# Transfer times in a hand-planned order: one queue accounted by bytes, big loads in pieces, deeper weight staging, gate operands split in place

## The chip, the core and the metric

The kernel runs on one core of one Trainium2 chip. The metric is the device time of one execution in microseconds; the time before is the median of three runs. Engines are named as in the profile: PE is the matrix engine, ACT and DVE are the two elementwise engines, POOL does almost nothing here, and SP issues all the transfers, on one queue and in program order. Every engine works through its own list of instructions in order, so an instruction that waits holds back all that stands behind it on that engine.

## The reference

The input x is 4 sequences of 3072 rows with 256 channels. Three stages follow one another.

```
# 1: mixing in the frequency domain, along the sequence
X  = rfft(x, axis=1)
Yr = Xr @ w_r - Xi @ w_i + b_r ;  Yi = Xr @ w_i + Xi @ w_r + b_i
Y  = soft_threshold(Yr, 0.01) + 1j * soft_threshold(Yi, 0.01)
x  = irfft(Y)
# 2: two dense layers, 256 -> 2048 -> 256 (w_in, w_out)
h = x @ w_in ;  x = (h * tanh(softplus(h))) @ w_out
# 3: channel mix over the token before, 256 -> 1024 -> 256 (w_k, w_v), gate (w_r of its own)
x_prev = x shifted by one row
k = relu((mu_k*x + (1-mu_k)*x_prev) @ w_k)
r = sigmoid((mu_r*x + (1-mu_r)*x_prev) @ w_gate)
out = r * ((k*k) @ w_v)
```

The weights of stages 2 and 3 come as 64-bit floats and are decoded on the chip.

## The kernel before, in words

**Number format.** A matrix product is done in three passes: each operand is split into a rounded high part (a copy on ACT) and a low part (a subtraction on DVE), and high×high, high×low and low×high are added up. All elementwise helpers have one line each: `tt` (L201) and `stt` (L204) on DVE, `act` (L207) on ACT, `mm` (L210) on PE.

**Part 1** (stage 1, L650) is 48 steps u, 12 for each sequence b. A step runs a forward transform (`emit_F`, tile xps), the channel mix (`emit_M`, yps) and an inverse transform (`emit_I`, bps) on PE, with the evacuations `post_F` (xh, xl), `post_M` (yb) and `post_I` (bs, stored to b_dr) between them. The combining of 24 rows before and after lies on DVE: `f1_ops` ahead, `f3_ops` behind. `f3_ops` (L330) loads one half of a sequence from b_dr into the tile g (1536 KB, L334 to L337), runs about 46 DVE operations in place and stores to y_dr. For sequence 0 it runs inside part 1, for the others in part 2.

**Weight staging.** In steps 36 to 47 the weights of stage 2 are loaded in 16 pieces of 512 KB (`raw_piece`, L497; tile raw, three buffers), decoded on DVE and ACT (`decode`, L503) and split. A pipeline (`Weights`, L591) takes two pieces in a step: `vec` issues the DVE part, `sca` the ACT part and the load of a later piece, so that at most `depth` pieces lie loaded and not yet begun (L841: three at the start; L875, L880: two later). The first eight pieces belong to w_in; each pair of them is widened to seven matrices for a seven-product scheme (`pair_pieces`, L558), split into a staging tile (yc in the trace) and stored to h_dr by two stores of 896 KB (L583), 14 rows of 512 bytes in each partition. The last eight belong to w_out and stay on the chip (wo). The weights w_k are staged the same way in steps 6 to 14 (tile wst).

**Part 2** (stages 2 and 3, L908) works on 12 superblocks J of 1024 tokens. Stage 2 has 8 groups of hidden columns for each superblock (96 groups), stage 3 has 4 (48 groups). A group (`group`, L932) makes seven products of 128×512 tiles in banks x, z, c, d, sums on DVE (k), activations on ACT (h) and low parts on DVE (l); the second layer's product of a group (`unit_H`, `unit_K`; banks a and v) follows one group later. The 384 loads of first-layer weights (`load_ring`, L645; tile wr) go into two rings of four tiles; a load waits until the group two earlier has used its tile.

**The order** of part 2 is written by a planner (`Plan`, L97). Each step has an engine, a hold time, a due time and the steps it needs. The planner keeps one clock for each engine; when an engine is free in its account, it emits of the steps whose needs are met in that account the one with the earliest due time, early or not. A step is done after its hold, a hand-over time (`AFTER`, L101) and, for transfers, a landing time:

```
AFTER = {"PE": 0.2, "ACT": 0.19, "DVE": 0.16, "POOL": 0.3, "SP": 0.0, "-": 0.0}
last = add("SP", 0.1, t0, load, prev, land=9.0)      # f3_job: 1536 KB
```

A transfer thus holds SP for 0.1 or 0.2 us in the account, whatever its size. The account decides only the order; on the chip the engines wait for each other by semaphores. The steps on SP are: `load_ring`; the source tiles of the next superblock (`moving`, L1054: ysrc or xsrc, 1 MB by two transfers in one step, then four sums on DVE and seven splits); the loads and stores of `f3_job` (L1078); the stores of the shifted mixes (L1143, xk_dr and xr_dr through four tm buffers); the decoding of w_v and the gate's weight (dec, L1154 on, five pieces in sequence); the fetch of the weights of stage 3 (L1194, wk and wv); the gate's operand (`gate_prep`, L1254: 1 MB into xrf, split into xr); and the stores of the result. The gate (`gate`, L1280, bank z, tile r) runs four times a superblock, one in each group of stage 3, and in the first superblock two in group 2 and two in group 3.

Of the kernel before, what the change touches and what calls it, by code (L numbers as in the profile page):

```python
# [25 lines left out]
NB = 4  # L26
# [70 lines left out]
class Plan:  # L97
# [3 lines left out]
    AFTER = {"PE": 0.2, "ACT": 0.19, "DVE": 0.16, "POOL": 0.3, "SP": 0.0, "-": 0.0}  # L101
# [67 lines left out]
def tile_fft_mix_moe_channel_mix(  # L169
# [160 lines left out]
    def f3_ops(b, h):  # L330
# [3 lines left out]
        def load():  # L334
            G = g_p.tile([128, 32, 128], F32, tag="g", name="g")
            st["G"] = G
            nc.sync.dma_start(out=G[:, 0:24, :], in_=b_dr[b][h].rearrange("p t (r f) -> p (t r) f", r=2))  # L337

# [138 lines left out]
    def load_mix(h):  # L477
        raw = pools["st"].tile([128, 2, 256], F32, tag="raw", name="wraw", bufs=3)
# [18 lines left out]
    def raw_piece(src):  # L497
        raw = pools["st"].tile([128, 512, 2], I32, tag="raw", name="raw", bufs=3)
# [59 lines left out]
    def pair_pieces(w, dst, i, m, field, stage):  # L558
# [8 lines left out]
        def second():  # L567
            a0, v0, v1, a2, v2, a1 = decode(raw_piece(w[:, 256 * (i + m):256 * (i + m) + 256]),
                                            lambda: f["s"][:, 4:7:2, :], lambda q: [])
            s = lambda k: f["s"][:, k, :]  # L570

# [4 lines left out]
            def highs():  # L576
                t = f["t"] = stage()
                return [lambda: act(t[:, 0:4, 0, :], f["s"][:, 0:4, :], ACTF.Copy),
                        lambda: act(t[:, 4:7, 0, :], f["s"][:, 5:8, :], ACTF.Copy)]

            def lows():
                t = f["t"]
                put = lambda g: nc.sync.dma_start(  # L583
                    out=dst[2 * i + g], in_=t.rearrange("p m s f -> p (m s) f")[:, :, 128 * g:128 * g + 128].bitcast(F32))
                return [lambda: tt(t[:, 0:4, 1, :], f["s"][:, 0:4, :], t[:, 0:4, 0, :].bitcast(F32), SUB),
                        lambda: tt(t[:, 4:7, 1, :], f["s"][:, 5:8, :], t[:, 4:7, 0, :].bitcast(F32), SUB),
# [30 lines left out]
    def load_y(j):  # L617
        b, o = divmod(j, 3)
        t = src_p.tile([128, 8, 512], F32, tag="src", name="ysrc")
        for h in range(2):  # L620
            nc.sync.dma_start(out=t[:, 6 - 2 * h:8 - 2 * h, :].rearrange("p i f -> p (i f)"),
                              in_=y_dr[b][h, :, 8 * o:8 * o + 8, :].rearrange("p n f -> p (n f)"))
        return t
# [26 lines left out]
    def part1():  # L650
        with ExitStack() as es:
# [169 lines left out]
            for u in range(NU):  # L821
# [9 lines left out]
                if u == NU - NT - 1:  # L831
                    mv[0] = big.tile([128, 2, 7, 512], F32R, tag="big", name="yc")
                    flat = mv[0].rearrange("p a b f -> p (a b f)")
                    half = [flat[:, 3584 * i:3584 * i + 3584].rearrange("p (m s f) -> p m s f", m=7, s=2) for i in range(2)]
# [6 lines left out]
                    wq.load(3)  # L841
# [3 lines left out]
                elif PARK_AT[0] <= u < PARK_AT[1]:  # L845
                    dec = 1
                    if u == PARK_AT[0]:
                        wfield = src_p.tile([128, 2, 8, 256], F32, tag="src", name="wsrc")
                        todo = []
                        for i in range(2):  # L850
                            todo += pair_pieces(w_k, k_dr, i, 2, lambda i=i: wfield[:, i],
                                                lambda: g_p.tile([128, 7, 2, 256], F32R, tag="g", name="wst"))
# [21 lines left out]
                if dec:  # L874
                    emit(wq.sca(2))  # L875
                if u > 1:
                    post_I(u - 2)
                if dec == 2:
                    emit(wq.vec())
                    emit(wq.sca(2))  # L880
# [8 lines left out]
                if b == NB - 1:  # L889
                    if t == 6:  # L890
                        ysrc = load_y(0)
# [6 lines left out]
            while wq.busy():  # L898
                emit(wq.vec())
                emit(wq.sca(2))  # L900
# [7 lines left out]
    def part2():  # L908
        with ExitStack() as es:
# [76 lines left out]
            def outs_of(second, off, f32_of, hi_of, unit_of, cost):  # L986
# [65 lines left out]
            out_H = outs_of(units, 0, f32_H, None, unit_H, 1.362)  # L1052

            def moving(key, b0, pace, load, old, *prev):  # L1054
# [4 lines left out]
                def get():  # L1059
                    tl["s"] = load()  # L1060
                ld = add("SP", 0.2, b0, get, *prev, land=7.0)
# [33 lines left out]
            for J in range(NSB):  # L1095
# [5 lines left out]
                if J + 1 < NSB:  # L1101
                    old = [p for g in range(8) for p in prods[8 * (J - 1) + g]] if J else None
                    yprep[J + 1], src_reads = moving(J + 1, B0 + 8, 6.0, lambda J=J: load_y(J + 1), old,
                                                     src_reads, f3_of.get((J + 1) // 3))
# [269 lines left out]
```

## Time and profile before

| | |
|---|---|
| Median of 3 runs | 1937.7 us (1934.22 to 1941.81) |
| The profiled execution: time | 1939.15 us |
| The profiled execution: span of its instructions | 1937.4 us |
| PE busy, DVE busy, ACT busy | 1878.8, 1397.8, 1210.2 us |
| Granted PE clock, mean | 0.992 of full |
| Transfers | 255.66 MB, 41.8% of 16 DMA engines' time |

In views over time, the number after a start time is a duration, and brackets hold the idle time of that engine just before, with what ended it. Lines with SPq are the issuing of a transfer, not its duration. Part 1 runs to about 342 us, stage 2 to about 1345 us, stage 3 to the end.

### The profile page before, as it was taken

The page shows a single profiled execution, that of the slowest core. Times are in us where ns is not written, and L with a number is a line of the kernel's source. Part 1 is how long each engine was busy: PE and PEld are TensorE (multiplying, and loading weights), DVE is VectorE, ACT ScalarE, POOL GpSimd, SP SyncE. Part 2 cuts the span into 40 slices and gives each one's busy share as a digit, 9 for nine tenths or more (in the row PEclk, how much of TensorE's full clock was granted, in tenths as well). Part 3 has the DMA queues.
Part 4 walks back from the last instruction along what each step waited for, and adds up shares of the span by engine and source line. Part 5 has one row for each costly group of instructions (what it writes and reads, how often), then busy time and mean ns, then how long its engine had stood idle before and what let it go on. Part 6 is the DMA issues. An engine that isn't in the chain of part 4 may idle for free.

```text
span 1937.4 us, 26749 instructions
## 1 busy us (share of the span) xinstructions
PE 1878.8 (97%) x9654; PEld 1611.2 (83%) x9654; DVE 1397.8 (72%) x2565; ACT 1210.2 (62%) x2141; POOL 7.6 (0%) x16
## 2 busy tenths in 40 slices
PE   6999989898999998999999999999999999999999
PEld 5888877687878887778888888888899999999998
DVE  8999976697988895766747567575666666666654
ACT  2432276565657577875757667575777777777765
POOL 0000000000000000000000000000000000000000
PEclk9999999999999999999999999999999999999999
DMA  9455186456456554544434344353412222211201
GB/s 285 128 171 174 54 266 194 160 175 212 139 174 209 155 166 148 187 137 128 155 90 155 106 142 155 90 180 91 168 66 67 69 76 70 70 66 66 75 25 34
DMA packets 197539, 255.66 MB, mean 132 GB/s; under 512 B 15128, under 2 KB 126368, under 8 KB 196384
## 3 DMA queue, kind: packets, MB, share of 16 engines
q1 hardware_dynamic: 197408, 253.96, 41.8%
q8 instruction: 77, 1.26, 0.3%
q14 instruction: 54, 0.44, 0.1%
HBM read 177.35 MB, written 76.55 MB: 131 GB/s over the span
## 4 chain that ended last, share of the span: by engine, by line
PE 87%; DVE 4%; DMA 4%; ACT 4%; issue 1%; SPq 0%; ACTq 0%; DVEq 0%
PE a L210 25%; PE x L210 14%; PE v L210 13%; PE c L210 10%; PE yps L210 5%; PE z L210 5%; PE d L210 5%; PE zps L210 3%; PE bps L210 3%; PE xps L210 3%; DMA raw<-in_moe_w_out_dram 1%; DMA wr<-h_dr 1%; ACT L207 1%; DVE a L201 1%; ACT k L207 1%
## 5 line engine op out<-in xcount | busy, mean ns | idle before, releaser
L201 DVE TENSOR_TENSOR l<-k,h 128x512 fp32r<-128x512 f32 x576 | 385.3, 686 | 376.3 <-ACT h L207 203.6
L210 PE MATMUL a<-h,wo 128*128 128x512 f32 x1536 | 531.9, 390 | 0.0
L210 PEld LDWEIGHTS a<-h,wo 128*128 128x128 f32 x1536 | 289.5, 189 | 60.5
L210 PE MATMUL a<-l,wo 128*128 128x512 f32 x768 | 299.9, 391 | 5.8 <-DVE l L201 5.8
L210 PE MATMUL v<-wv,h 128*128 128x256 f32 x1536 | 278.2, 280 | 0.0
L207 ACT ACTIVATE c<-x 128x512 f32<-128x512 f32 x288 | 168.6, 586 | 157.8 <-PE x L210 153.4
L210 PEld LDWEIGHTS v<-wv,h 128*128 128x128 f32 x1536 | 247.5, 190 | 13.8
L210 PE MATMUL x<-yc,wr 128*128 128x512 f32 x864 | 244.8, 392 | 3.9 <-ACT c L207 3.5
L207 ACT ACTIVATE k<-k 128x512 f32<-128x512 f32 x288 | 177.1, 632 | 69.9 <-DVE k L201 67.7
L210 PE MATMUL v<-wv,l 128*128 128x256 f32 x768 | 215.3, 280 | 0.0
L210 PEld LDWEIGHTS x<-yc,wr 128*128 128x128 f32 x864 | 162.4, 189 | 40.8 <-ACT c L207 5.6
L207 ACT ACTIVATE k<-c 128x512 f32<-128x512 f32 x288 | 172.1, 598 | 33.6 <-PE c L210 18.0
L210 PE MATMUL c<-yc,wr 128*128 128x512 f32 x576 | 164.1, 393 | 13.1 <-DVE k L201 13.1
L207 ACT ACTIVATE d<-x 128x512 f32<-128x512 f32 x144 | 84.2, 585 | 146.8 <-PE x L210 146.8
L210 PEld LDWEIGHTS a<-l,wo 128*128 128x128 f32 x768 | 144.8, 189 | 36.3 <-DVE l L201 6.2
L210 PEld LDWEIGHTS v<-wv,l 128*128 128x128 f32 x768 | 144.6, 188 | 0.0
L207 ACT ACTIVATE h<-k 128x512 fp32r<-128x512 f32 x192 | 117.5, 629 | 42.4 <-DVE k L204 40.5
L210 PEld LDWEIGHTS c<-yc,wr 128*128 128x128 f32 x576 | 108.1, 189 | 38.5 <-DVE k L201 16.4
L201 DVE TENSOR_TENSOR k<-c,zs 128x512 f32<-128x512 f32 x144 | 99.1, 688 | 51.6 <-ACT c L207 48.6
L210 PE MATMUL x<-yc,wk 128*128 128x512 f32 x432 | 124.1, 396 | 0.0
L201 DVE TENSOR_TENSOR g<-g 128x128 f32<-128x128 f32 (+3 forms) x272 | 110.0, 432 | 1.4 <-DMA wr<-h_dr 0.4
L210 PE MATMUL bps<-im,yb 128*128 128x256 f32 x384 | 93.3, 387 | 10.5 <-DVE yb L204 10.5
(105 smaller groups left out, 2823.1 us busy)
## 6 DMA issues: line engine op xcount, KB each, us to landing
wr<-h_dr SPq DMA_DIRECT2D x288, 256.0 KB, 2.7
b_dr<-bs SPq DMA_DIRECT2D x48, 256.0 KB, 2.2
g<-b_dr SPq DMA_DIRECT2D x8, 1536.0 KB, 7.0
ysrc<-y_dr SPq DMA_DIRECT2D x24, 512.0 KB, 4.6
wr<-h_dr SPq DMA_DIRECT2D x96, 128.0 KB, 2.1
xk_dr<-tm SPq DMA_DIRECT2D x48, 256.0 KB, 3.1
xr_dr<-tm SPq DMA_DIRECT2D x48, 256.0 KB, 3.2
xsrc<-xk_dr SPq DMA_DIRECT2D x24, 512.0 KB, 4.2
```

Of the source, the lines that this page charges most:

```text
L201: V.tensor_tensor(out=o, in0=a, in1=b, op=op)
L207: S.activation(out=o, in_=i, func=f, **kw)
L210: T.matmul(out=o, lhsT=l, rhs=r, start=start, stop=stop, **kw)
```

## The change

In the planner's account, transfers hold SP for about the time of their bytes (1.2 us for 256 KB, 2.6 us for 512 KB) and land later; hand-over times grow to 0.25 us. The 1536 KB load of `f3_job` is issued as four pieces, each a planner's step; source tiles and the gate's operand are loaded by two steps instead of one. `f3_job`'s DVE operations are due 12 us later. The fetch of stage 3's weights is due later and more slowly. Weight staging has four raw buffers, four pieces loaded at the start and three ahead in steps 36 to 47; the staging tile's layout becomes [2, 7, 2, 128], so that each of the two stores reads one row of 7168 bytes in each partition. The gate's operand is loaded straight into the half of xr that will hold the low part, ACT copies the high part out of it and DVE subtracts in place; it no longer uses the tile xrf, and its load waits for the last superblock's gates instead. In the first superblock of stage 3 it is due earlier and all four gates stand in group 3.

```diff
-    AFTER = {"PE": 0.2, "ACT": 0.19, "DVE": 0.16, "POOL": 0.3, "SP": 0.0, "-": 0.0}
+    AFTER = {"PE": 0.25, "ACT": 0.25, "DVE": 0.25, "POOL": 0.3, "SP": 0.0, "-": 0.0}
...
-        def load():
-            G = g_p.tile([128, 32, 128], F32, tag="g", name="g")
...
+        def load(k=None):
+            if not k:
+                st["G"] = g_p.tile([128, 32, 128], F32, tag="g", name="g")
+            t0, t1 = (0, 12) if k is None else (3 * k, 3 * k + 3)
+            nc.sync.dma_start(out=st["G"][:, 2 * t0:2 * t1, :],
+                              in_=b_dr[b][h][:, t0:t1, :].rearrange("p t (r f) -> p (t r) f", r=2))
...
-        raw = pools["st"].tile([128, 512, 2], I32, tag="raw", name="raw", bufs=3)
+        raw = pools["st"].tile([128, 512, 2], I32, tag="raw", name="raw", bufs=4)
...
+            part = lambda t, a, b, w: t[:, :, a:b, w, :].rearrange("p g m f -> p m g f")
+            pair = lambda a, b: f["s"][:, a:b, :].rearrange("p m (g f) -> p m g f", g=2)
...
-                put = lambda g: nc.sync.dma_start(
-                    out=dst[2 * i + g], in_=t.rearrange("p m s f -> p (m s) f")[:, :, 128 * g:128 * g + 128].bitcast(F32))
...
+                put = lambda g: nc.sync.dma_start(out=dst[2 * i + g], in_=t[:, g].rearrange("p m s f -> p (m s) f").bitcast(F32))
+                return [lambda: tt(part(t, 0, 4, 1), pair(0, 4), part(t, 0, 4, 0).bitcast(F32), SUB),
...
-                    wq.load(3)
+                    wq.load(4)
...
-                    emit(wq.sca(2))
+                    emit(wq.sca(3 if b == NB - 1 else 2))
...
-                ld = add("SP", 0.2, b0, get, *prev, land=7.0)
+                ld = [add("SP", 2.6, b0, lambda: get(0), *prev, land=8.0)]
+                ld.append(add("SP", 2.6, b0 + 3, lambda: get(1), ld, land=8.0))
...
-                last = add("SP", 0.1, t0, load, prev, land=9.0)
+                last = [add("SP", 2.0, t0 + 3 * k, lambda k=k: load(k), prev, land=8.0) for k in range(4)]
...
-                    due = t0 + 10 + w * k / len(ops)
+                    due = t0 + 22 + w * k / len(ops)
...
-                        stores.append(add("SP", 0.1, due, fn, last, land=3.0))
+                        stores.append(add("SP", 0.5, due, fn, last, land=8.0))
...
-                        wl = [add("SP", 0.1, at(n) - 1.8 * T_H + 0.2 * k * T_H, lambda n=n, k=k: load_ring(n, k),
-                                  old and old[2 * k:2 * k + 2], land=3.5) for k in range(4)]
+                        wl = [add("SP", 1.2, at(n) - 1.8 * T_H + 0.2 * k * T_H, lambda n=n, k=k: load_ring(n, k),
+                                  old and old[2 * k:2 * k + 2], land=4.0) for k in range(4)]
...
-                        st = add("SP", 0.1, due + 2, lambda t=t, dst=dst, J=J, w=w, h=h, i=i: nc.sync.dma_start(
-                            out=dst[J][1 - h if w == 0 else h, :, 512 * i:512 * i + 512], in_=t), v, land=3.0)
+                        st = add("SP", 1.2, due + 2, lambda t=t, dst=dst, J=J, w=w, h=h, i=i: nc.sync.dma_start(
+                            out=dst[J][1 - h if w == 0 else h, :, 512 * i:512 * i + 512], in_=t), v, land=5.0)
...
-                ld = add("SP", 0.1, due, begin, prev, land=5.0)
+                ld = add("SP", 2.6, due, begin, prev, land=8.0)
...
-                order = add("SP", 0.1, at(NA - 6) + e, fetch, free, dec_done, order)
-                have[w, g, k] = add("-", 0.0, 0.0, lambda: None, order, land=3.5)
+                order = add("SP", 1.3, at(NA - 4) + 2 * e, fetch, free, dec_done, order)
+                have[w, g, k] = add("-", 0.0, 0.0, lambda: None, order, land=5.0)
...
-                ld = add("SP", 0.2, b0, load, xk_done[1, J], xr_reads or mix_prev, land=7.0)
...
+                        nc.sync.dma_start(out=xr[0][:, 1, :, s].bitcast(F32), in_=xr_dr[J].rearrange("h p f -> p h f")[:, :, s])
+                    ld = add("SP", 2.6, b0 + 18 * i, load, xk_done[1, J], dec_done, first,
+                             [r_units[J - 1, 2 * i + m] for m in range(2)] if J else None, land=8.0)
...
+                        a = add("ACT", 0.54, b0 + 12 + 18 * i + 2 * h, lambda hi=hi, lo=lo: act(hi(), lo().bitcast(F32), ACTF.Copy), ld)
+                        v = add("DVE", 0.6, b0 + 14 + 18 * i + 2 * h, lambda hi=hi, lo=lo: tt(
+                            lo(), lo().bitcast(F32), hi().bitcast(F32), SUB), a)
...
-                due = at(NA + 4 * J + need[0]) + 0.6 * T_K
+                due = at(NA + 4 * J + need[0]) + (0.6 if J else 0.2 + 0.2 * q) * T_K
...
-                xrp, xr_reads = gate_prep(J, at(n0) - (0.5 if J == 0 else 2.5) * T_K)
+                xrp = gate_prep(J, at(n0) - (8 * T_H if J == 0 else 2.5 * T_K))
...
-                    for q in ({0: [0], 1: [1], 2: [2], 3: [3]} if J else {2: [0, 1], 3: [2, 3]}).get(g, []):
+                    for q in [g] if J else range(4) if g == 3 else []:
```

The decoding's store (2.6 us, landing 8), the stores of the result (1.2 us, landing 4) and the load of `load_y`, now one half at a time, are changed in the same way.

## Rows read from the trace of the kernel before

**Rows 1.** The page's first part: busy time, share of the span and instructions of each engine.

```profile
PE 1878.8 (97%) x9654; PEld 1611.2 (83%) x9654; DVE 1397.8 (72%) x2565; ACT 1210.2 (62%) x2141; POOL 7.6 (0%) x16
```

**Rows 2.** Waits of PE: line, releaser, us in total, times, longest.

```profile
PE c L210 <- DVE k L201: 17.0, 7, 5.6
...
PE bps L210 <- DVE yb L204: 10.5, 6, 3.7
PE a L210 <- DVE l L201: 5.8, 1, 5.8
```

**Rows 3.** Timeline of PE in the weight staging: starts of three steps.

```profile
263.14 1.89 PE L210 MATMUL xps<-fm,a 128*128 128x256 f32 x8
...
316.43 1.89 PE L210 MATMUL xps<-fm,a 128*128 128x256 f32 x8
...
322.84 1.89 PE L210 MATMUL xps<-fm,a 128*128 128x256 f32 x8
```

**Rows 4.** Timeline of DVE in the weight staging: first operation of each step's pieces.

```profile
259.09 0.42 DVE L517 TENSOR_SCALAR wsrc<-raw 128x512 int32<-128x512 int32 x1
...
267.22 0.42 DVE L517 TENSOR_SCALAR wsrc<-raw 128x512 int32<-128x512 int32 x1
...
276.17 0.43 DVE L517 TENSOR_SCALAR wsrc<-raw 128x512 int32<-128x512 int32 x1 [0.74 <-DMA raw<-in_moe_w_in_dram]
...
285.68 0.43 DVE L517 TENSOR_SCALAR q<-raw 128x512 int32<-128x512 int32 x1 [1.30 <-DMA raw<-in_moe_w_out_dram]
...
294.28 0.43 DVE L517 TENSOR_SCALAR q<-raw 128x512 int32<-128x512 int32 x1 [1.98 <-DMA raw<-in_moe_w_out_dram]
...
304.68 0.43 DVE L517 TENSOR_SCALAR q<-raw 128x512 int32<-128x512 int32 x1 [4.32 <-DMA raw<-in_moe_w_out_dram]
```

**Rows 5.** Windows: stretch, length, busy of PE, PEld, DVE, ACT, POOL, clock, DMA share, GB/s.

```profile
267.50:271.50 4.00, 2.97 (x14) 2.27 (x13) 3.93 (x8) 3.10 (x5) 0.00 (x0) 1.00 1.01 286
303.00:305.00 2.00, 0.00 (x0) 0.00 (x0) 0.32 (x1) 0.39 (x1) 0.00 (x0) 1.00 1.07 401
359.00:364.00 5.00, 4.92 (x15) 3.98 (x16) 5.00 (x8) 3.30 (x8) 0.00 (x0) 0.66 0.02 9
484.00:490.00 6.00, 5.98 (x17) 4.76 (x18) 6.00 (x14) 3.00 (x5) 0.00 (x0) 0.61 0.18 48
1373.00:1379.00 6.00, 5.56 (x17) 4.69 (x18) 4.28 (x8) 4.55 (x9) 0.00 (x0) 0.50 0.55 149
```

**Rows 6.** Timeline, part 2's start and superblock 1: DVE stalls and SP's issues.

```profile
357.73 0.69 DVE L201 TENSOR_TENSOR ysrc<-ysrc 128x512 f32<-128x512 f32 x1 [6.17 <-DMA ysrc<-y_dr]
...
464.72 0.32 SPq L337 DMA_DIRECT2D g<-b_dr  x1
465.13 0.94 SPq L621 DMA_DIRECT2D ysrc<-y_dr  x2
...
478.47 2.02 DVE L201 TENSOR_TENSOR ysrc<-ysrc 128x512 f32<-128x512 f32 x3 [8.57 <-DMA ysrc<-y_dr]
```

**Rows 7.** The decoding of w_v: timeline of DVE and PE; group of ACT's table loads.

```profile
739.45 0.43 DVE L1169 TENSOR_SCALAR dec<-dec 128x512 int32<-128x512 int32 x1 [3.52 <-DMA wr<-h_dr]
...
748.18 1.65 PE L210 MATMUL c<-yc,wr 128*128 128x512 f32 x3 [4.56 <-DVE k L201]
...
L207 ACT ACT_TABLE_LOAD x15 | 19.2, 1283 | 9.5 <-DMA braw<-in_b_r_dram 9.3
```

**Rows 8.** Timeline, change from stage 2 to stage 3: ACT and PE.

```profile
1369.84 0.72 ACT L207 ACTIVATE tm<-x2s,mus 128x512 f32<-128x512 f32 x1 [4.43 <-DMA xk_dr<-tm]
...
1373.44 1.65 PE L210 MATMUL c<-yc,wk 128*128 128x512 f32 x3 [3.98 <-DVE k L201]
...
1393.02 1.69 PE L210 MATMUL zps<-wk,xr 128*128 128x256 f32 x12 [0.50 <-ACT r L207]
```

**Rows 9.** Issues of one line: g by tile (first and last start); wr with us to landing.

```profile
L337 SPq DMA_DIRECT2D g<-b_dr x6: 319/320/423, 345.3 to 662.8; - x6
...
wr<-h_dr SPq DMA_DIRECT2D x288, 256.0 KB, 2.7
```

More of the change, by code (lines that the diff above doesn't have):

```diff
@@ L477, in load_mix @@
     def load_mix(h):
-        raw = pools["st"].tile([128, 2, 256], F32, tag="raw", name="wraw", bufs=3)
+        raw = pools["st"].tile([128, 2, 256], F32, tag="raw", name="wraw", bufs=4)
         nc.sync.dma_start(out=raw[:, 0, :], in_=w_r[128 * h:128 * h + 128, :])
@@ L615, in sca, with load_y @@
             return ops + [lambda: self.load(depth)]
-    def load_y(j):
+    def load_y(t, j, h):
         b, o = divmod(j, 3)
[L619 to L623, printed above, removed]
+        nc.sync.dma_start(out=t[:, 6 - 2 * h:8 - 2 * h, :].rearrange("p i f -> p (i f)"),
+                          in_=y_dr[b][h, :, 8 * o:8 * o + 8, :].rearrange("p n f -> p (n f)"))
     SUMS = [(0, 7, 5, ADD), (1, 0, 6, SUB), (2, 6, 7, SUB), (3, 4, 1, SUB)]
@@ L833, in part1 @@
                     flat = mv[0].rearrange("p a b f -> p (a b f)")
-                    half = [flat[:, 3584 * i:3584 * i + 3584].rearrange("p (m s f) -> p m s f", m=7, s=2) for i in range(2)]
+                    half = [flat[:, 3584 * i:3584 * i + 3584].rearrange("p (g m s f) -> p g m s f", g=2, m=7, s=2) for i in range(2)]
                     wfield = src_p.tile([128, 2, 8, 256], F32, tag="src", name="wsrc")
@@ L879, in part1 @@
                     emit(wq.vec())
-                    emit(wq.sca(2))
+                    emit(wq.sca(3 if b == NB - 1 else 2))
                     bg.clock += 2100
@@ L890, in part1 @@
                     if t == 6:
-                        ysrc = load_y(0)
+                        ysrc = src_p.tile([128, 8, 512], F32, tag="src", name="src")
+                        for h in range(2):
+                            load_y(ysrc, 0, h)
                     prep(t)
@@ L899, in part1 @@
                 emit(wq.vec())
-                emit(wq.sca(2))
+                emit(wq.sca(3 if b == NB - 1 else 2))
             post_M(NU - 1)
@@ L984, in group, with outs_of @@
                 return [m1, m5, m6, m2, m7, m3, m4]
-            def outs_of(second, off, f32_of, hi_of, unit_of, cost):
+            def outs_of(second, off, f32_of, unit_of, cost):
                 def outs(n, made):
@@ L1177, in part2 @@
                 v4 = add("DVE", 0.6, due + 16, lambda: tt(lo_(), q_(), hi_().bitcast(F32), SUB), a4)
-                st = add("SP", 0.1, due + 17, lambda i=i: nc.sync.dma_start(
-                    out=v_dr[i], in_=sl(2048, 3072).rearrange("p (s f) -> p s f", s=2)), v4, land=5.0)
+                st = add("SP", 2.6, due + 17, lambda i=i: nc.sync.dma_start(
+                    out=v_dr[i], in_=sl(2048, 3072).rearrange("p (s f) -> p s f", s=2)), v4, land=8.0)
                 prev = [st, v4]
@@ L1254, in gate_prep @@
-            def gate_prep(J, b0):
-                tl = {}
-                def load():
-                    tl["f"] = x_p.tile([128, 2, 1024], F32, tag="s0", name="xrf")
-                    nc.sync.dma_start(out=tl["f"], in_=xr_dr[J].rearrange("h p f -> p h f"))
-                ld = add("SP", 0.2, b0, load, xk_done[1, J], xr_reads or mix_prev, land=7.0)
-                res, reads = {}, []
-                for i in range(2):
-                    for h in range(2):
-                        s = slice(512 * i, 512 * i + 512)
-                        def hi(h=h, s=s):
-                            if not xr:
-                                xr[0] = g_p.tile([128, 2, 2, 1024], F32R, tag="g", name="xr")
-                            act(xr[0][:, 0, h, s], tl["f"][:, h, s], ACTF.Copy)
-                        def lo(h=h, s=s):
-                            tt(xr[0][:, 1, h, s], tl["f"][:, h, s], xr[0][:, 0, h, s].bitcast(F32), SUB)
-                        a = add("ACT", 0.54, b0 + 12 + 18 * i + 2 * h, hi, ld, dec_done, reads[0:1],
-                                [r_units[J - 1, 2 * i + m] for m in range(2)] if J else None)
-                        v = add("DVE", 0.6, b0 + 14 + 18 * i + 2 * h, lo, a)
@@ L1334, in store @@
                             nc.sync.dma_start(out=out[b, t0:t0 + 256, :].rearrange("(q p) d -> p q d", p=128), in_=r_t[0][:, q])
-                        r_free[q] = add("SP", 0.1, due + 1, store, fin, land=3.0)
+                        r_free[q] = add("SP", 1.2, due + 1, store, fin, land=4.0)
                         fins[J, i].append(fin)
```

44 lines of the change are left out of this document (23 added, 21 removed).

## The prediction

> **What bounds the kernel now.** I read the page's busy shares first: PE is busy for 1878.8 of 1937.4 us [rows 1], so the instructions that the change leaves alone hold the time, and all that can be won lies in 58.6 us of idle PE and in the slow clock that follows idle stretches. The waits of PE come next: 10.5 us in part 1 behind the threshold (yb), 5.8 us once behind a low part (l) and 17.0 us in seven waits behind the sums k [rows 2]; most of the rest stands ahead of the first product and is not touched. Seven waits in 144 groups also say that the planner's order is sound nearly everywhere. The timelines then show what held DVE or ACT. In each large case an instruction waited for a transfer that the planner had taken for landed, and the product's sums stood behind it on the same engine. The windows add the clock: after such a stop PE runs partly at 1.2 instead of 2.4 GHz, its mean grant being 0.66, 0.61 and 0.50 in three stretches of 5 to 6 us [rows 5].
>
> **Weight staging.** Six steps of part 1 take 316.43 − 263.14 = 53.3 us, where a step without staging takes 322.84 − 316.43 = 6.41 [rows 3]: 14.8 us lost, clock included. DVE waited 0.74 + 1.30 + 1.98 + 4.32 = 8.3 us for raw pieces [rows 4]. But transfers are not the only bound: from 259.09 to 267.22 DVE worked without a wait on one step and took 8.13 us, and the next two passes take 8.95 − 0.74 and 9.51 − 1.30, 8.21 each; the two after them 6.6 and 6.1 [rows 4]. Against 6.41 the three widening passes are 1.7 + 1.8 + 1.8 too long and the fourth 0.2: 5.5 us, of which I take 0.7 as a reserve that is spent first (an estimate: one sum's length, 0.69 us [rows 6]). Thus 4.8 us stay whatever the transfers do, and at most 10.0 can come back.
>
> How much does come back hangs on bytes. A widening step moves two pieces (1.05 MB), two stores (1.84 MB) and 0.26 MB for b_dr. With the stores alone on the engines the window shows 286 GB/s, with piece loads 401, both at a full DMA share [rows 5]. At those rates a step needs 6.4 + 3.3 = 9.7 us, 1.5 more than DVE's pass; over four steps the transfers fall 6 us behind. One more piece ahead is worth half a pass, 4.1 us. So depth alone leaves 1.9 us and brings 8.1. If the long rows lift the stores to 401 GB/s, a step needs 7.9 us, less than DVE's 8.2, and all 10.0 come back. The row of the stores is 512 bytes, that of the pieces 2 KB, the new one 7 KB, so the faster rate is the nearer one; but a store need not follow a load. The Trainium skill ("DMA: Bandwidth & Descriptors", Specifications) puts the line rate at 512 bytes and more, which speaks against any gain from the longer rows; by it this part would bring 8.1 us. The 286 against 401 GB/s [rows 5] does not agree with it. I take 9.0, ends 0 (depth useless, should the queue serve in order and only shift the wait) and 10.0. That ACT and DVE now write runs of 128 elements costs nothing that I can find; the number of instructions and elements is unchanged.
>
> **Start of part 2 and superblock 1.** At 357.73 and 478.47 DVE had stood 6.17 and 8.57 us on the first sum of a source tile. In the second case SP issued 1536 KB for g at 464.72 and the source tile right behind it at 465.13 [rows 6]; the account called it landed 7.2 us later, the chip 13.3. The low part and the sums stood behind it: PE lost 5.8 us in the one and 5.6 in the other [rows 2], and of clock 5.0 × 0.34 = 1.7 and 6.0 × 0.39 = 2.3 [rows 5]: 7.5 and 7.9. In the new account the pieces of g hold SP for 8 us, the two halves of the source follow one another with 10.6 us each, so the sums are emitted some 20 us after the first issue and later than the data. I take 7.0 and 7.5; ends 0 and the full sums. What is late next: the sums and splits of the source, needed only a superblock (82 us) later; and `f3_job`, which starts 12 us or more later each time. Its six loads run from 345.3 to 662.8, 63.5 us apart [rows 9]; 15 us more for each makes the last of them end some 90 us later, near 820, and its tokens are wanted in superblock 8, after 990. That slack covers it; without it a whole load and its chain would stand open. The 18 more issues at 0.32 us [rows 9] lie on SP, which mostly waits for PE.
>
> **Decoding of w_v.** DVE stood 3.52 us on dec's first load and PE lost 4.56 at 748.18 [rows 7]. ACT also reloads its tables, 15 times 1.28 us in the whole run [rows 7]; I put most of them here, because dec's functions stand between those of stage 2. The longer landing removes the first, not the second. I take 3.0, ends 0 and 4.6. The other waits behind k, 17.0 − 5.6 − 4.56 − 3.98 = 2.9 us, I leave where they are (ends 0 and 2.9).
>
> **Stage 2 to stage 3.** ACT stood 4.43 us on a tm buffer whose store lay behind the weights' fetch, and PE lost 3.98 us [rows 8] and 6.0 × 0.50 = 3.0 of clock [rows 5], 7.0 together. Fetch and stores now have their time in the account, and the gate's 1 MB leaves this stretch. I take 5.0, ends 0 and 7.0.
>
> **What the change adds.** All four gates of the first superblock stand in group 3 and share one bank: between two of them PE waits for the sigmoid, as once before, 0.50 us [rows 8]. Three such waits are 1.5 us, which I charge; ends 0 and, if PE had nothing else to do for as long as a gate takes, 3 × 1.69 = 5.1. The gate's load now waits for gates of the superblock before: the later half can go after its fourth gate, with about 19 us to the gate that needs it, more than the account's 10.6 and two splits. Cost nothing; without that cover 11 superblocks would each pay. Behind the waiting load on SP stand only the stores of results and source tiles that are a superblock early. In place or not, a split is one copy and one subtraction. The longer hand-over times change no instruction; a chain of six links grows by some 0.4 us inside a group of 10.2, and two groups run interleaved: nothing.
>
> **The sum.** 9.0 + 7.0 + 7.5 + 3.0 + 5.0 − 1.5 = 30.0. Against the profiled execution's 1939.15 us that is 1909.15; the median stands 1.45 below that execution, which gives 1907.7.
>
> **The rivals.**
>
> *Bytes bind.* The same transfers lie ahead of the same data, so a stall is shortened only. Staging gains the 4.1 us of the extra piece, the two g cases half (3.8 and 4.0), the last change 2, the gates cost 1.5: 12.4 us, 1925.3. For it speak the full DMA share in staging [rows 5]; against it, that after 303 the engines ran at 401 GB/s with DVE waiting for a single piece. Chance 0.14.
>
> *The account does not reach the chip.* Steps may be issued in nearly the old order, since SP waits for PE's products most of the time; only the staging, which the planner does not order, improves: 9.0 us, 1928.7. Against it: in the old account 1536 KB and 1 MB land after 9 and 7 us however they are stacked, and that is just what fails in rows 6. Chance 0.07.
>
> *Slower: the ring tiles come late.* In the new account a superblock of 82 us holds SP for 32 × 1.2 (ring) + 8 × 1.2 (tm) + 5.2 (source) + 1.3 jobs × 11 (g) = 67 us, 82%. If bunching brings it to 100%, due loads queue and the planner emits products after them late, in an order that no longer interleaves. A ring load has 18.4 us of lead for 5.2 in the account and 2.7 on the chip [rows 9]; it decides from a delay of 13 us. The price is a late tile in each of the 38 groups beside the six jobs; at 0.8 us each it eats the 30 us, at 1.5 us the time is 1939.15 − 1.45 − 30 + 57 = 1964.7. Chance 0.07.
>
> **How the numbers follow.** My forecast keeps 0.72. Its own range comes from the ends: all upper ends, 10.0 + 7.5 + 7.9 + 4.6 + 2.9 + 7.0 = 39.9, give 1897.8; a shortfall of 10 gives 1917.7. The range for 8 in 10 adds the first rival and a little below for waits not listed: 1895 to 1926. A measurement can tell about 0.5%, 9.7 us, so faster means below 1928.0: nearly all of the forecast and most of the first rival, 0.83; the second rival and the rest of the first are the same, 0.10; slower 0.07.
>
> **What would show it.** Right: PE's waits behind yb fall to under 6 us, and DVE's waits on raw vanish; no DVE or ACT wait of several us on ysrc, dec or tm; stores of h_dr in a window above 286 GB/s; g issued four at a time with wr between. Wrong: DVE still idle on raw (bytes bind), new PE waits on wr or wk (ring late), on r in group 3, or PE waits of the old size behind k at new places.

## The result, and the profile after

| | before | after |
|---|---|---|
| Median (this batch: 4 runs each) | 1935.96 us (1933.55 to 1941.81) | 1906.26 us (1905.29 to 1907.51) |
| Ratio, 95% interval | | 0.9843 [0.9818, 0.9867] |
| The profiled execution: time, span | 1939.15, 1937.4 us | 1906.75, 1904.9 us |
| PE busy, PE idle within the span | 1878.8, 58.6 us | 1868.0, 36.9 us |
| Granted PE clock, mean | 0.992 | 0.998 |

The change takes off 29.7 us of the median, where 30.0 had been forecast, and 32.5 us of the span between the two profiled executions: 21.7 us of PE's idle time and 10.8 us of its busy time, though PE runs the same 9654 products. The total came out almost exactly, the parts less so: the decoding lost time where a gain was forecast, and the gates cost none where 1.5 us had been charged.

The page's busy line of after, which answers to [rows 1], and then the waits of PE (line, releaser, us in total, times, longest), which answer to [rows 2]:

```profile
PE 1868.0 (98%) x9654; PEld 1603.6 (84%) x9654; DVE 1412.8 (74%) x2565; ACT 1210.7 (64%) x2143; POOL 9.1 (0%) x16
```

```profile
PE xps L210 <- DVE g L201: 17.7, 2, 16.3
PE x L210 <- ACT c L207: 8.7, 7, 2.0
PE bps L210 <- DVE yb L204: 4.2, 4, 1.4
PE c L210 <- DVE k L201: 1.7, 2, 0.9
PE a L210 <- DVE l L201: 0.4, 1, 0.4
```

The first line is the start and was not touched. Behind the threshold (yb) 10.5 us became 4.2, behind k 17.0 became 1.7, behind l 5.8 became 0.4. The second line grew: seven waits for ACT of up to 2.0 us, where before had four, 3.5 us together, of up to 1.4. The windows (stretch, length, busy of PE with its products, clock, DMA share, GB/s) show where it sits:

```profile
420.00:520.00 100.00, 100.00 (x443) 1.00 0.54 168
520.00:800.00 280.00, 280.00 (x1237) 1.00 0.55 167
800.00:1050.00 250.00, 240.49 (x1037) 0.99 0.48 150
1050.00:1326.23 276.23, 276.23 (x1219) 1.00 0.45 140
1326.23:1400.00 73.77, 73.77 (x482) 1.00 0.33 110
```

From 420 us to the end of the change of stages PE stands still nowhere but between 800 and 1050 us, where w_v and the gate's weight are decoded. Put together by place (idle time from such windows of both traces; clock from [rows 5], for the staging what the starts of its steps leave beside the idle time, for the decoding from slices of 10 us; one trace of each kernel):

| place | forecast | idle gained | clock gained |
|---|---|---|---|
| weight staging (A) | 9.0 | 6.3 | 3.7 |
| start of part 2 (B) | 7.0 | 5.1 | 1.7 |
| superblock 1 (C) | 7.5 | 5.6 | 2.3 |
| 520 to 700 us (one wait for ACT's c, one behind k) | 0 | 1.9 | not resolved |
| decoding (E) | 3.0 | −0.8 | −1.6 |
| stages 2 to 3 (F), with the gates | 5.0 − 1.5 | 4.5 | 3.0 |
| start, not touched | 0 | −0.9 | 0 |

The idle column adds up to the 21.7 us; the clock column to 9.1 of 10.8, and the remaining 1.7 us of busy time has no place that the records show.

**Staging.** The timeline of PE in after, the same steps as [rows 3]:

```profile
264.07 1.89 PE L210 MATMUL xps<-fm,a 128*128 128x256 f32 x8
...
278.07 1.99 PE L210 MATMUL bps<-im,yb 128*128 128x256 f32 x8 [1.41 <-DVE yb L204]
...
286.19 1.99 PE L210 MATMUL bps<-im,yb 128*128 128x256 f32 x8 [1.42 <-DVE yb L204]
...
307.41 1.89 PE L210 MATMUL xps<-fm,a 128*128 128x256 f32 x8
```

Six steps take 43.34 us instead of 53.3; against 6 × 6.41 that leaves a loss of 4.9 us, where the prediction had a floor of 4.8. What is left are waits for DVE's passes of 8.12 us, not for transfers: in the same stretch DVE never waits for raw. Timeline of DVE in after, the first operation of two passes (compare [rows 4]):

```profile
268.15 0.42 DVE L519 TENSOR_SCALAR wsrc<-raw 128x512 int32<-128x512 int32 x1
...
276.27 0.42 DVE L519 TENSOR_SCALAR wsrc<-raw 128x512 int32<-128x512 int32 x1
```

The stores of h_dr are also issued faster. Timeline of SP, one step of after (L586) and the same step of before (L583):

```profile
274.19 0.81 SPq L586 DMA_DIRECT2D h_dr<-yc  x2
```

```profile
273.26 4.24 SPq L583 DMA_DIRECT2D h_dr<-yc  x2
```

**The order.** SP in after at the start of part 2: g in pieces, with ring loads between, as the prediction said. The source's first half stands behind three of the four pieces, the last piece follows it. The next four pieces of g, at 413.47 us, stand in a row.

```profile
336.30 0.42 SPq L338 DMA_DIRECT2D g<-b_dr  x1
336.81 0.38 SPq L646 DMA_DIRECT2D wr<-h_dr  x1
337.25 0.42 SPq L338 DMA_DIRECT2D g<-b_dr  x1
...
339.47 0.56 SPq L621 DMA_DIRECT2D src<-y_dr  x1
...
343.12 0.42 SPq L338 DMA_DIRECT2D g<-b_dr  x1
```

After 320 us neither DVE nor ACT waits for any transfer: the 14.7 us of DVE on the source, the 13.6 us of ACT on tm's stores and the waits on dec are gone. `f3_job`'s last load starts at 744.0 us instead of 662.8 and its last store at 807.7 (forecast: near 820), before its tokens are wanted.

### The profile page after: what moved, and what is told of

It is laid out like the page before. It is cut to its first block, busy times and chain, and to the rows that moved or that the text cites. A ratio compares the mean times of both kernels' runs of the same rounds, so it can differ in the third digit from the quotient of the medians.

```text
span 1904.9 us, 26716 instructions
## 1 busy us (share of the span) xinstructions
PE 1868.0 (98%) x9654; PEld 1603.6 (84%) x9654; DVE 1412.8 (74%) x2565; ACT 1210.7 (64%) x2143; POOL 9.1 (0%) x16
## 4 chain that ended last, share of the span: by engine, by line
PE 88%; ACT 5%; DVE 5%; DMA 1%; issue 1%; SPq 0%; ACTq 0%; DVEq 0%
PE a L210 24%; PE x L210 14%; PE v L210 14%; PE c L210 10%; PE yps L210 5%; PE d L210 5%; PE z L210 5%; PE zps L210 4%; PE bps L210 3%; PE xps L210 3%; ACT k L207 1%; ACT L207 1%; DVE wsrc L204 1%; DVE a L201 1%; ACT tm L207 1%
## 5 line engine op out<-in xcount | busy, mean ns | idle before, releaser
L201 DVE TENSOR_TENSOR l<-k,h 128x512 fp32r<-128x512 f32 x576 | 393.0, 692 | 333.0 <-ACT h L207 164.6
L210 PE MATMUL a<-h,wo 128*128 128x512 f32 x1536 | 522.8, 390 | 0.0
L201 DVE TENSOR_TENSOR k<-d,zs 128x512 f32<-128x512 f32 x144 | 99.1, 688 | 48.8 <-PE d L210 48.4
L201 DVE TENSOR_TENSOR yc<-src,yc 128x512 fp32r<-128x512 f32 x168 | 112.6, 690 | 16.9 <-ACT yc L207 16.0
```

Source lines behind the costliest of these rows:

```text
L201: V.tensor_tensor(out=o, in0=a, in1=b, op=op)
L210: T.matmul(out=o, lhsT=l, rhs=r, start=start, stop=stop, **kw)
```

## The experiments

Every kernel was timed beside before in its own batch; ratios are to before, whose own median lay between 1935.6 and 1937.1 us in these batches, so a difference of 1 us between kernels of two batches says little.

| kernel | median, us | ratio, 95% interval |
|---|---|---|
| after | 1906.26 | 0.9843 [0.9818, 0.9867] |
| depth_back | 1909.11 | 0.9856 [0.9837, 0.9874] |
| rows_back | 1910.43 | 0.9865 [0.9849, 0.9882] |
| account_back | 1923.16 | 0.9930 [0.9909, 0.9951] |
| before_account | 1920.25 | 0.9916 [0.9901, 0.9931] |
| gate_back | 1910.18 | 0.9867 [0.9850, 0.9883] |
| one_piece | 1907.77 | 0.9855 [0.9839, 0.9872] |
| handover_back | 1903.93 | 0.9836 [0.9821, 0.9851] |
| before_no_tables | 1924.05 | 0.9937 [0.9924, 0.9950] |
| dec_no_tables | 1891.17 | 0.9768 [0.9754, 0.9783] |
| dec_copies | 1890.79 | 0.9761 [0.9747, 0.9774] |
| sums_on_pool | 1888.88 | 0.9754 [0.9741, 0.9768] |
| pool_dec_handover | 1888.10 | 0.9749 [0.9735, 0.9763] |

### Depth and long rows, each taken back (depth_back, rows_back)

```diff
# depth_back, on after
-        raw = pools["st"].tile([128, 512, 2], I32, tag="raw", name="raw", bufs=4)
+        raw = pools["st"].tile([128, 512, 2], I32, tag="raw", name="raw", bufs=3)
-                    wq.load(4)
+                    wq.load(3)
-                    emit(wq.sca(3 if b == NB - 1 else 2))
+                    emit(wq.sca(2))
# rows_back, on after: the staging tile [7, 2, 256] and its two stores as in before
-    put = lambda g: nc.sync.dma_start(out=dst[2 * i + g], in_=t[:, g].rearrange("p m s f -> p (m s) f").bitcast(F32))
+    put = lambda g: nc.sync.dma_start(
+        out=dst[2 * i + g], in_=t.rearrange("p m s f -> p (m s) f")[:, :, 128 * g:128 * g + 128].bitcast(F32))
```

> The changed kernel with three raw buffers and the old depth (three pieces at the start, two ahead), long rows kept. If the extra piece does the work, as the prediction has it (8.1 of 10.0 us), DVE waits for raw pieces again in three or four of the six steps, 1 to 3 us each, and the time is 3 to 8 us above the changed kernel's 1906.3: 1909 to 1914. If the long rows alone cure the staging, DVE's waits on raw stay under 1 us in all and the time is within 1 us of 1906.3.

> The changed kernel with the old layout of the staging tile (14 rows of 512 bytes for each partition and store), the new depth kept. By the prediction's sum the stores fall back to some 290 to 350 GB/s and the staging loses 1.9 us more: 1908.2, with DVE waits on raw of about 2 us in all. If rows of 512 bytes run at the same rate as long ones, nothing changes: 1906.3, no waits, stores at the same GB/s. If the rows did most of the work, 1911 or more.

Six steps take 46.21 us in depth_back (a loss of 7.75) and 49.57 us in rows_back (11.1), against 4.9 with both and 14.8 with neither. So in these traces the long rows alone bring 7.1 us and the depth alone 3.7. The old staging itself scatters, though: in before_account and before_no_tables below, which don't touch it, it lost 12.3 and 13.1 us instead of 14.8. The order of the two is safe, their sizes only to some 2.5 us. In the times, taking the depth back costs 2.9 us and the rows 4.2; these intervals overlap each other and that of after. DVE's waits on raw, in depth_back and then in rows_back (line, releaser, us in total, times, longest):

```profile
DVE q L519 <- DMA raw<-in_moe_w_out_dram: 3.1, 2, 2.6
```

```profile
DVE q L519 <- DMA raw<-in_moe_w_out_dram: 5.3, 2, 3.9
```

What the rows change is seen in the windows while the stores alone are on the engines (columns as in [rows 5]), in after and then in rows_back:

```profile
268.00:272.00 4.00, 2.97 (x15) 2.24 (x13) 3.93 (x8) 2.67 (x4) 0.00 (x0) 1.00 1.05 339
```

```profile
268.00:272.00 4.00, 2.97 (x14) 2.27 (x14) 3.93 (x8) 3.17 (x5) 0.00 (x0) 1.00 1.01 285
```

The engines are fully busy in both, at 339 and 285 GB/s (360 and 286 in windows that start half a us earlier: a window of 4 us holds few rows of 7 KB); over 264 to 300 us the mean is 365 against 309 GB/s. The Trainium skill ("DMA: Bandwidth & Descriptors", Specifications) puts the line rate at transfers of 512 bytes and more; the stores with rows of 512 bytes don't reach the rate of those with 7 KB here, and the measurement decides.

### The account, taken back and alone (account_back, before_account)

```diff
# account_back, on after: every hold, landing and hand-over time as in before; all pieces and places stay
-    AFTER = {"PE": 0.25, "ACT": 0.25, "DVE": 0.25, "POOL": 0.3, "SP": 0.0, "-": 0.0}
+    AFTER = {"PE": 0.2, "ACT": 0.19, "DVE": 0.16, "POOL": 0.3, "SP": 0.0, "-": 0.0}
-    wl = [add("SP", 1.2, at(n) - 1.8 * T_H + 0.2 * k * T_H, lambda n=n, k=k: load_ring(n, k),
-              old and old[2 * k:2 * k + 2], land=4.0) for k in range(4)]
+    wl = [add("SP", 0.1, at(n) - 1.8 * T_H + 0.2 * k * T_H, lambda n=n, k=k: load_ring(n, k),
+              old and old[2 * k:2 * k + 2], land=3.5) for k in range(4)]
...
# before_account, on before: only the new numbers, the whole of g as one step of 8.0, a source as one of 5.2
-    last = add("SP", 0.1, t0, load, prev, land=9.0)
+    last = add("SP", 8.0, t0, load, prev, land=8.0)
...
```

> The changed kernel with all hold, landing and hand-over times of the old account (0.1 us of SP for each transfer); pieces, split source loads, depth, rows and the gate's new place kept. If the account is what cured part 2, stops of several us on the source tile and on tm come back and the time is 15 to 20 us above 1906.3: 1921 to 1926. If loading in pieces cured it, 5 us at most: up to 1911.

> The kernel before with only the account's numbers changed (g holds SP for 8 us in one step, a source tile or the gate's operand for 5.2); no pieces, old staging, old gate. If the account alone cures part 2, the three large stops after 340 us are gone, the staging still loses 14.8 us and the time is 16 to 20 us under the kernel before: about 1916 to 1920. If pieces are needed, a ring tile or the source tile waits behind the 1536 KB and the time is 1925 or more.

Taking the account back costs 16.9 us, putting it alone into before brings 16.5. In account_back the waits on the source and on tm's stores return (first fence: waits of DVE, second: waits of ACT) and with them PE's stops at the old places (timeline: the start of part 2, superblock 1, the change of stages):

```profile
DVE src L201 <- DMA src<-y_dr: 15.8, 3, 8.2
```

```profile
ACT tm L207 <- DMA xk_dr<-tm: 12.5, 10, 3.9
```

```profile
348.79 1.65 PE L210 MATMUL x<-yc,wr 128*128 128x512 f32 x3 [4.44 <-ACT c L207]
...
481.74 1.65 PE L210 MATMUL c<-yc,wr 128*128 128x512 f32 x3 [3.52 <-DVE k L201]
...
1360.66 1.04 PE L210 MATMUL c<-yc,wk 128*128 128x512 f32 x3 [3.46 <-DVE k L201]
```

Before_account has none of the three. It has neither the pieces nor the later due times of `f3_job` and of the weights' fetch, and account_back has both: so it is the account's numbers that cure these stops. In before_account the staging is still slow (a loss of 12.3 us), at the first gates three stops of 2.4 us together have come, and in the decoding it has a stop as long as the one it lost, 3.99 us at 856.83, now for ACT. That was the first sign that the decoding's stop was not the transfer's.

### Small parts (gate_back, one_piece, handover_back)

```diff
# gate_back, on after: the gate's operand through xrf, its due time and places as in before
-                    for q in [g] if J else range(4) if g == 3 else []:
+                    for q in ({0: [0], 1: [1], 2: [2], 3: [3]} if J else {2: [0, 1], 3: [2, 3]}).get(g, []):
# one_piece, on after
-                last = [add("SP", 2.0, t0 + 3 * k, lambda k=k: load(k), prev, land=8.0) for k in range(4)]
+                last = add("SP", 8.0, t0, load, prev, land=8.0)
# handover_back, on after: AFTER alone as in before
-    AFTER = {"PE": 0.25, "ACT": 0.25, "DVE": 0.25, "POOL": 0.3, "SP": 0.0, "-": 0.0}
+    AFTER = {"PE": 0.2, "ACT": 0.19, "DVE": 0.16, "POOL": 0.3, "SP": 0.0, "-": 0.0}
```

In one_piece the source's two halves are one step of 5.2 as well.

> The changed kernel with the gate's operand as before (tile xrf, one load of 1 MB due half a group ahead, first superblock's gates two in group 2 and two in group 3), with that load's time in the account. If the gate's new place matters as the kernel before with only the account suggests, PE waits of about 2.4 us around the first gates return and the time is 2 to 4 us above 1906.3: 1908 to 1910. If the prediction's charge of 1.5 us for four gates in one group were right, the time falls to 1905. If the gate is hidden either way: within 1 us of 1906.3.

> The changed kernel with the 1536 KB load and the source tile each as one planner's step again (8.0 and 5.2 us of SP in the account, one and two transfers). If the account is what counts, ring tiles have 18 us of lead and nothing waits: within 2 us of 1906.3. If the pieces were needed, ring or source tiles come late behind 1536 KB, with waits of 2 us and more: 1910 or more.

> The changed kernel with the old hand-over times (0.20, 0.19 and 0.16 us instead of 0.25), transfers' times kept. The prediction gives them no price: within 1 us of 1906.3. If the longer hand-overs do part of the work, PE waits behind k or c grow by 2 us or more in all and the time is 1908 or more.

gate_back stands 3.9 us above after, with intervals that overlap. Its trace has three stops that after hasn't, 2.3 us together (timeline of PE, first superblock of stage 3, and of ACT ahead of it):

```profile
1370.47 1.69 PE L210 MATMUL zps<-wk,xr 128*128 128x256 f32 x12 [0.93 <-ACT r L207]
...
1372.84 0.97 PE L210 MATMUL z<-yc,wk 128*128 128x512 f32 x3 [0.69 <-ACT r L207]
...
1374.50 1.70 PE L210 MATMUL zps<-wk,xr 128*128 128x256 f32 x12 [0.69 <-ACT zs L207]
```

```profile
1366.31 2.19 ACT L207 ACTIVATE xr<-xrf 128x512 fp32r<-128x512 f32 x4 [1.76 <-DMA xrf<-xr_dr]
```

ACT stands on the late load of xrf, splits all four parts in a row and only then comes to the sigmoids. So the run takes back the place, the time of the load and the tile together, and does not tell which of them costs the 2.3 us.

In after the gates stand apart with first-layer products between them, and none waits:

```profile
1362.27 1.52 PE L210 MATMUL zps<-wk,xr 128*128 128x256 f32 x12
1363.63 0.86 PE L210 MATMUL c<-yc,wk 128*128 128x512 f32 x3
...
1369.19 1.57 PE L210 MATMUL zps<-wk,xr 128*128 128x256 f32 x12
```

The pieces of g and of the source are worth nothing that can be measured (1.5 us, within both intervals): what helps is that the account knows the bytes, not that they come in parts. The longer hand-over times cost 2.3 us if anything, more than the 1 us expected, and that too lies within the intervals.

### The decoding's table loads (dec_no_tables, before_no_tables, dec_copies)

The stops that after has left stand beside table loads of ACT. Timeline of PE in after, the first of the seven, and of ACT ahead of it:

```profile
846.33 0.96 PE L210 MATMUL x<-yc,wr 128*128 128x512 f32 x3 [1.97 <-ACT c L207]
```

```profile
838.53 1.28 ACT L207 ACT_TABLE_LOAD   x1
839.83 1.15 ACT L207 ACTIVATE dec<-dec 128x512 f32<-128x512 int32 x2
841.00 1.28 ACT L207 ACT_TABLE_LOAD   x1
842.29 1.15 ACT L207 ACTIVATE k<-k 128x512 f32<-128x512 f32 x2
```

The decoding's Sign and Abs have one table, stage 2's Mish another; the two operations take 1.15 us together and cost two loads of 1.28 us each besides. In the runs of this part they stand on DVE, with the same result (the sign of an integer by a maximum with −1 and a minimum with 1, the absolute value as the larger of q and −q):

```diff
-                a2 = add("ACT", 0.54, due + 8, lambda: act(sg(), sg().bitcast(I32), ACTF.Sign), a1)
+                a2 = add("DVE", 0.36, due + 8, lambda: V.tensor_scalar(
+                    out=sg(), in0=sg().bitcast(I32), scalar1=-1.0, scalar2=1.0, op0=ALU.max, op1=ALU.min), a1)
...
-                a3 = add("ACT", 0.54, due + 10, lambda: act(q_(), q_(), ACTF.Abs), v2)
+                a3 = add("DVE", 0.6, due + 10, lambda: stt(q_(), q_(), -1.0, q_(), MULT, ALU.max), v2)
# dec_copies has besides, behind each of the two:
+                a2 = add("ACT", 0.54, due + 9, lambda: act(sg(), sg(), ACTF.Copy), a2)
...
+                a3 = add("ACT", 0.54, due + 11, lambda: act(q_(), q_(), ACTF.Copy), a3)
```

> The changed kernel with the sign and the magnitude of the decoding of w_v taken on DVE instead of ACT, so that ACT's function tables are not reloaded between stage 2's functions (14 of its loads, 18 us of ACT). If the table loads make the stops of 1.97, 0.95, 0.85 and 1.99 us that are left in part 2, those are gone and the time falls by 5 to 6 us, to about 1901. If these stops come from ACT's crowding at the superblock's edge alone, two of about 1.5 us stay and the time falls by 2 us at most: 1904.5.

> The kernel before with the sign and the magnitude of the decoding of w_v taken on DVE, nothing else changed. If ACT's table loads made most of the stops between 740 and 840 us (8.6 us of idle PE and some 1.7 us of clock), the time falls by 6 to 8 us, to 1928 to 1930. If the transfer that DVE waited 3.5 us for made them, as the prediction's 3.0 us has it, the stop of 4.56 us stays at 3 us or more and the time falls by 4 us at most.

> The changed kernel with the decoding's Sign and Abs on DVE, as in the faster version at 1891.2 us, but with a Copy on ACT put in behind each of the two, in place: ACT has its ten operations of 0.63 us back, and DVE keeps its ten extra ones, so that the table loads alone are missing (17 before, 3 expected). Theory 1, the table loads themselves (14 times 1.28 us, in front of stage 2's activations) make PE's seven stops: the time stays at 1891 to 1893 us and PE does not stop between 800 and 1050 us. Theory 2, ACT is merely too full there, and it was the ten operations taken off ACT that helped: some 6.3 of the 24.3 us of ACT work removed come back, with a longer chain for every piece, so that stops of 0.5 to 1 us return and the time is 1895 to 1900 us.

dec_no_tables takes off 15.1 us, more than I had expected: I had counted four stops where there are seven of 9.5 us together, and PE's busy time falls too, from 1868.0 to 1861.0. dec_copies gives ACT ten operations back, as copies, and keeps the time, so in after it is the loads and not the operations. Its group of table loads (after has 17) and its windows of PE:

```profile
L207 ACT ACT_TABLE_LOAD x3 | 3.8, 1283 | 9.5 <-DMA braw<-in_b_r_dram 9.4
```

```profile
700.00:800.00 100.00, 100.00 (x443) 1.00 0.53 159
800.00:1050.00 250.00, 250.00 (x1105) 1.00 0.50 158
```

In 800 to 1050 us PE now does 1105 products where after did 1037. before_no_tables shows the same for the kernel before: 11.9 us less, where 6 to 8 had been expected. In before the stop of 4.56 us [rows 7] had three table loads ahead of it, the last at 744.88 (timeline of ACT, then of DVE, in before): the sums k stood on DVE behind an operation of the decoding that waited for ACT.

```profile
744.88 1.28 ACT L207 ACT_TABLE_LOAD   x1
```

```profile
746.84 0.69 DVE L204 SCALAR_TENSOR_TENSOR dec<-dec 128x512 f32<-128x512 f32 x1 [1.25 <-ACT dec L207]
```

In before_no_tables DVE still stands on dec's first transfer, even for longer than in [rows 7], and PE has one stop of 0.84 us behind it (timeline of DVE and of PE; windows of PE):

```profile
735.87 0.43 DVE L1170 TENSOR_SCALAR dec<-dec 128x512 int32<-128x512 int32 x1 [4.11 <-DMA wr<-h_dr]
```

```profile
737.00 0.97 PE L210 MATMUL x<-yc,wr 128*128 128x512 f32 x3 [0.84 <-ACT d L207]
```

```profile
700.00:880.00 180.00, 179.07 (x789) 1.00 0.53 165
```

Before had 739 products in that stretch and 8.7 us of idle PE; here 0.9 are left, and the slices of 0.90 and 0.92 behind the old stop, 1.8 us of clock, are at 1.00. These 9.6 us are what the decoding gave back. The rest of the difference lies elsewhere: in this trace the stop in superblock 1 is 2.90 us instead of 5.64, though the edit stands behind it in the program. That the loads and not ACT's ten operations did it is shown for after alone.

### What is left of the staging (sums_on_pool, pool_dec_handover)

```diff
# sums_on_pool, on dec_no_tables; pool_dec_handover has the old AFTER too
-                return v1() + [lambda: tt(s(1), s(4), s(0), SUB), lambda: tt(s(2), s(6), s(1), SUB),
-                               lambda: tt(s(5), s(6), s(4), SUB), lambda: tt(s(7), s(3), s(2), SUB)]
+                pt = lambda o, a, b: P.tensor_tensor(out=o, in0=a, in1=b, op=SUB)
+                return v1() + [lambda: pt(s(1), s(4), s(0)), lambda: pt(s(2), s(6), s(1)),
+                               lambda: pt(s(5), s(6), s(4)), lambda: pt(s(7), s(3), s(2))]
```

> The kernel dec_no_tables (1891.2) with the four widening sums of each pair of w_in and w_k pieces on POOL instead of DVE. If DVE's 8.2 us for a step are the bound that is left in the staging, a pass falls to some 6.5 us, the three PE stops of 1.0, 1.4 and 1.4 us are gone and the time falls by 3 to 5 us, to 1886 to 1888. If POOL's sums take so long that the copies and subtractions behind them wait, or slow DVE down beside them, PE stops stay and the time is 1891 or more.

> The kernel sums_on_pool with the old hand-over times as well. If they are without effect, as the prediction has it, it is within 1 us of sums_on_pool. If the 2.4 us that the run handover_back lay under the changed kernel are the hand-over times' own price, 2 to 3 us under sums_on_pool. If they only moved the table loads about, no difference now that those are gone.

The four sums of a widening pass on POOL bring 2.3 us, less than the 3 to 5 expected. Timeline of sums_on_pool: POOL's four sums of one pass, and three DVE operations of the same time.

```profile
274.00 3.82 POOL L577 TENSOR_TENSOR wsrc<-wsrc 128x256 f32<-128x256 f32 x4 [3.70 <-DVE wsrc L204]
```

```profile
274.29 1.12 DVE L204 SCALAR_TENSOR_TENSOR wsrc<-raw,wsrc 128x512 int32<-128x512 int32 x1
...
276.53 0.70 DVE L204 SCALAR_TENSOR_TENSOR wsrc<-wsrc,sg 128x512 f32<-128x512 f32 x1
277.15 0.95 DVE L519 TENSOR_SCALAR wsrc<-raw 128x512 int32<-128x512 int32 x1
```

DVE is rid of four sums, 1.56 us, and still needs 7.5 us for a pass instead of 8.1, because operations that take 0.69 and 0.42 us alone take 1.12 and 0.95 beside POOL's: 0.96 of the 1.56 us are lost again. The three stops behind yb shrink from 1.0 to 1.4 us to 0.4 to 0.8. With the old hand-over times on top the time is 1888.10 us, within the interval of sums_on_pool: the fastest version tried, 18 us under after and 48 under before.

## Why the prediction was right, and where not

**A, staging: total right, shares wrong.** 9.9 us came back where I had taken 9.0 and bounded it by 10.0; against the other two traces of the old staging it would be 7.4 and 8.2. The floor of DVE's passes held to 0.1 us, partly by chance: the passes were 8.12 us instead of 8.21, and the reserve 0.4 us instead of 0.7. But the step "depth alone leaves 1.9 us and brings 8.1" falls: depth alone brings 3.7 and the rows alone 7.1. Both of its terms were off. I had the transfers fall 6 us behind; DVE's waits on raw in the three traces of the old staging are 7.5 to 8.3 us. And I had taken one more piece for half a pass, 4.1 us; in rows_back DVE still waits 5.3 us, so the piece took off 2.2 to 3.0. The choice of the faster rate for 7 KB rows was right, and it carries the larger part.

**B, C and F: mechanism and size right.** The sums were emitted ahead of their data because transfers cost nothing in the account. B, C and F were put at 19.5 us, 18.0 with the charge for the gates, and gave 22.2 with the gates in them; account_back brings the three stops back and nothing in the staging. The rival that the account would not reach the chip is refuted by before_account. That bytes bind and stalls only get shorter is refuted by the trace of after, where DVE and ACT wait for no transfer behind 320 us; and that the ring loads would come late did not happen: no wait on wr or wk appears.

**The gates: a charge for nothing.** I had charged 1.5 us for three waits on the sigmoid; there is none in after, and the old arrangement (place, late load, xrf) has 2.3 us of stops under the new account. The failed step is "between two of them PE waits for the sigmoid": the planner put other products between, which is the end of 0 that I had named and not taken.

**E, the decoding: the wrong cause.** "The longer landing removes the first, not the second. I take 3.0" is half right: the wait for the transfer is gone from after, yet the idle time of the place went from 8.7 to 9.5 us. I had put the table loads down as a second cause and given the 4.56 us stop to the transfer. before_no_tables shows that the transfer's wait by itself costs PE 0.84 us at most, and that Sign and Abs on ACT were the cost in both kernels, 9.6 us at this place in before and 15.1 of the time in after. So the term of 3.0 us came out at −2.4, and this error of 5.4 us was made up by the gates, by clock in F and by the 1.9 us at 520 to 700 us that I had left at nothing. That the sum came within 0.3 us of the median's change is luck.

**Costed at nothing:** for the pieces one_piece bears it out, to 1.5 us. For the issues added on SP and the in-place split no wait shows in after, but no run takes them back alone. For the hand-over times the runs cannot tell 2 us; with the table loads gone, pool_dec_handover puts them at 0.8.

## What to carry to other kernels

Where an order is planned by an account, a transfer has to hold its queue for the time of its bytes; without that, what depends on it is emitted too early and stalls its engine for everybody behind it. When an instruction waits for a transfer and a product waits behind it, look on the same engine for what else is new there before giving the stop to the transfer: an activation of another table between those of the main loop costs two loads, and here it was cheaper to do Sign and Abs on DVE. A stop's price is its idle time and the slow clock after it, and both have to be read from the stretch.

## What the runs showed of the hardware

- **Short rows hold the queue, too.** Two stores of 896 KB with rows of 512 bytes kept SP in issuing for 1.9 us the first time and for 4.0 to 4.4 us the next three, in before and in rows_back; with rows of 7 KB each pair took 0.81 us.
- **A table load costs just its time here.** ACT's operation before the load at 838.53 ended at 838.52, the load took 1.28 us and the next operation began at 839.83. The Trainium skill ("ScalarE: Activation LUTs", What ACT_TABLE_LOAD costs) gives the same 1283 ns and a drain of 1380 ns with it; no such drain shows here.
- **Short stops cost clock, but not each of them.** After the stops of 1.96 and 1.99 us at 932.86 and 1021.00 the slices of 10 us have a grant of 0.83, after the one of 1.97 us at 846.33 it stays at 1.00:

```profile
930.00:940.00 10.00, 8.04 (x28) 0.83 0.31 85
1020.00:1030.00 10.00, 9.00 (x32) 0.83 0.36 109
```

  In depth_back, rows_back and gate_back, too, two of the three stops of 1.97 to 1.99 us have a slower grant behind them, and not always the same two. In after these two make 3.4 us of the 7.0 us of busy time that dec_no_tables saves; where the rest lies the records don't show.
- **Beside POOL's sums some DVE operations take longer, others don't.** DVE's 0.42 us become 0.95 and 0.69 become 1.12 beside POOL's sums of 0.95 us; the operation at 276.53 between them keeps its 0.70. The Trainium skill ("SBUF — State Buffer", SBUF: two separate sides) has DVE and GpSimd, which is POOL, share a pair of ports that one instruction holds for its whole length. The two longer operations agree with that; an experiment on the ports alone was not made.
